# A ring of 2560 instead of 2304 tokens, and 512-token blocks in slots 48 to 143, in a fused window-attention and two-layer kernel

## The chip, the cores and the metric

The kernel runs on one core of a Trainium2 chip. The metric is the device time of one execution in microseconds; lower is better. The profile is of one execution, and its times are microseconds from the start of its span, unless marked ns.

## The reference

Attention with a window of 32 tokens to each side, over 8 batches of 8 heads, 576 tokens and 64 elements, and then two matrix products with an activation between them on the 8 x 576 = 4608 tokens of 512 elements. Inputs and output are float32.

```python
scores = np.matmul(q, k.transpose(0, 1, 3, 2)) / np.sqrt(64)      # 8, 8, 576, 576
mask = np.abs(pos[:, None] - pos[None, :]) <= 32
scores = np.where(mask, scores, -1e9)
attn = np.exp(scores - scores.max(-1, keepdims=True))
attn = attn / (attn.sum(-1, keepdims=True) + 1e-9)
x = np.matmul(attn, v).transpose(0, 2, 1, 3).reshape(4608, 512)
h = x @ w_in                                                      # 512 x 2048
g = np.where(h >= 1, h, np.where(h <= -1, 0, (h + 1) ** 2 / 4))
return g @ w_out                                                  # 2048 x 512
```

## The kernel before

All matmuls take bfloat16 and sum in float32. The order of the work is written out by hand: each engine runs its instructions in the order in which the Python loop emits them, and semaphores keep data right between engines.

**The main loop** (`for a in range(NF * NB + 2 * NF)`) has 160 slots; `a` is the slot. In slots 0 to 143 a slot makes one tile of 512 elements per partition of the hidden layer, in this order:

- TensorE projects into `hp`, a PSUM tile of the pool `ps_h`, which has two buffers. A *narrow* slot takes 256 tokens and 256 of the 2048 hidden features: 8 matmuls of 256 columns (in `project`, L488). A *wide* slot takes 512 tokens and 128 features: 4 matmuls of 512 columns (L513), over the planes `kk` of `xT` in the order 0, 2, 1, 3. Slots 56 to 135 are wide (`WIDE = 56, 136`), so eight narrow slots make one block of 256 tokens, and sixteen wide slots make two.
- ScalarE makes `rr` from `hp` (L532), VectorE makes `mx` from `hp` and `rr` (L538) and `gT` from `rr` and `mx` (L539). In a few early slots ScalarE makes `mx`. When both have read `hp`, its buffer is free, for the projection two slots on.
- TensorE multiplies `gT` of earlier blocks with `w_out` into `op` (`unit`, L448): from slot 40 on three matmuls of 512 columns a slot, from slot 72 on four; slots before 40 take a part of this work in another form. Each 16 of them end a tile of 128 tokens, which ScalarE copies to `osb` (L452) and SyncE's queue stores.

**The input of the projection** is `xT`, the attention's output, transposed: four planes of 128 partitions, plane `kk = 2a + y`. It is a ring of `RING = 4 * S` = 2304 tokens: token n stands at n modulo 2304. `gT` has four places for blocks of 256 tokens; the function `home` says which place a block takes, so that the two blocks of a wide pair, which begins at an odd block, stand at a fixed step from each other.

**The attention** is cut into *sessions*, which the function `at` hangs on slots; `run(a)` emits those of slot `a` after the slot's projection, `run(a + 0.5)` those of `a + 0.5` after the slot's `unit` matmuls. A batch has five sums, each paired with scores that are needed later (`steps`): plane parity `y1` = 0 and 1 of tokens 0 to 223, the same of tokens 224 to 479, and tokens 480 to 575 of both. The list `sl` gives the slots of the sessions from the second sums of batch 2 on: entry n holds sums number 6 + n and scores number 7 + n of the sequence that begins with batch 1. Sums of batch 3 are entries 4 to 8, those of batch 4 entries 9 to 13. In a session

- TensorE makes the sums (matmuls of `pt` with `ones` and `vn` into `bb`, L294). `bb` is of the pool `ps_n`, which has one buffer; then the scores (L228, L253), into the one buffer of `ps_s`.
- ScalarE takes Exp of the scores (L236, or L261 for a batch's last scores, which are fewer), then Ln and Exp of the sums, the reciprocal (L300, L301: `lr`, `rc`).
- VectorE masks the exponentials (L202), and multiplies `bb` with `rc` into `xT` (L306, L309). These multiplies are collected in `muls`, and `flush()` emits them at the start of the next slot, ahead of that slot's `mx`. The multiply is the last reader of `bb`.

In the slots that concern us the order on every engine is therefore: projection, `rr`, `mx`, `gT`, then the session, then `unit`; or `unit` ahead of the session where it hangs on a half.

**The loads** of batches 3 to 7 (q, k and v through GpSimd's queue, `load_nat` and `load_v`), and the transposes of q and k by DMA from SyncE's queue (`xpose`), hang on slots counted from `sl`: the loads 17 to 15 slots ahead of the session `sl[5 * (b - 1) - 7]`, the transposes 11 and 9 slots ahead of it.

Of the kernel before, what the change touches and what calls it, by code (L numbers as in the profile page):

```python
# [14 lines left out]
def kernel(  # L15
# [19 lines left out]
    nc = tc.nc  # L35
    B, H, S, D = q.shape
# [3 lines left out]
    NU = NY * S // 128  # L40
    MAIN = 480
    TAIL = S - MAIN
    RING = 4 * S
    PAD = 32
    WIDE = 56, 136
    LONG = 2

    const = ctx.enter_context(tc.tile_pool(name="const", bufs=1))
# [20 lines left out]
    w_out = const.tile([128, 16, DM], BF, name="w_out")  # L69
    xT = const.tile([128, NY, RING], BF, name="xT")  # L70
    gT = const.tile([128, 16, 4, 256], BF, name="gT")
# [3 lines left out]
    V, P, A = nc.vector, nc.gpsimd, nc.scalar  # L75
# [73 lines left out]
    w = [(load_w_in, c0, c1, h) for c0, c1 in zip(cuts, cuts[1:]) for h in range(2)]  # L149
# [114 lines left out]
    muls = []  # L264

    def sums(b, y1, lo, hi, pool=ps_n):

        bb = two_banks(pool)
        w = hi - lo
        todo = []  # L270
        if lo < MAIN:
            ys, D0 = (y1,), w
            for par in range(2):
                a0 = max(lo, 32 * par)
                off = 32 - 64 * par
                todo.append((None, a0 - lo, hi - lo, lambda a, h, par=par, a0=a0, off=off: (
                    pt[b][HD[a], h, y1, par, a0 + off:hi + off])))
                for c2 in range(4):
                    q0, q1 = max(0, 128 * c2 - off, lo), min(128 * c2 + 128 - off, hi)
                    if q0 < q1:  # L280
                        todo.append((NC * y1 + 2 * c2 + par, q0 - lo, q1 - lo, lambda a, h, par=par, q0=q0, q1=q1, off=off: (
                            pt[b][HD[a], h, y1, par, q0 + off:q1 + off])))
        else:
            ys, D0 = (0, 1), 2 * w
            todo.append((None, 0, 2 * w, lambda a, h: pt8[b][HD[a], h].rearrange("p y j -> p (y j)")))
            for y in ys:
                todo.append((NC * y + 8, y * w, y * w + w, lambda a, h, y=y: pt8[b][HD[a], h, y]))
                for c in (None, NC * y + 7):
                    todo.append((c, y * w, y * w + 64, lambda a, h, y=y: pt[b][HD[a], h, y, 1, 448:512]))
        for n, (c, c0, c1, p) in enumerate(todo):  # L290
            o = D0 if c is None else 0
            for a in range(2):
                for h in range(2):
                    nc.tensor.matmul(bb[HD[h], a, o + c0:o + c1], ones[HD[a]] if c is None else vn[b][HD[a], c, h],  # L294
                                     p(a, h), start=n == 0, stop=True, skip_group_check=True)

        def end():
            lr = smp.tile([128, 2, 256], FP, name="lr", bufs=1)
            rc = smp.tile([128, 2, 256], FP, name="rc")
            A.activation(lr[:, :, :D0], bb[:, :, D0:2 * D0], AF.Ln)  # L300
            A.activation(rc[:, :, :D0], lr[:, :, :D0], AF.Exp, scale=-1.0)  # L301
            r0 = (b * S + lo) % RING
            o = xT.rearrange("p (a y) t -> p a y t", a=2)[:, :, ys[0]:ys[-1] + 1, r0:r0 + w]
            if len(ys) == 1:
                o = o[:, :, 0]
                muls.append(lambda: V.tensor_mul(o, bb[:, :, :D0], rc[:, :, :D0]))  # L306
            else:
                like = "p a (y j) -> p a y j"
                muls.append(lambda: V.tensor_mul(o, bb[:, :, :D0].rearrange(like, y=2), rc[:, :, :D0].rearrange(like, y=2)))  # L309
        return end  # L310
# [68 lines left out]
    NF = DFF // 256  # L379
# [27 lines left out]
        at(a, seq[2 + n][0])  # L407
    for n, a in enumerate((18, 20, 26.5, 28)):
        at(a, seq[3 + n][1])
    sl = [30, 32, 35, 38, 41, 44, 47, 50, 52, 57, 60, 63, 66, 68, 72, 76, 79, 82, 86]  # L410
    sl += [90, 93, 96, 100, 104, 108, 111, 114, 118, 123]
    for n, a in enumerate(sl):
        at(a, seq[6 + n][0], seq[7 + n][1] if n < len(sl) - 1 else None)
    for t in range(2):
# [2 lines left out]
    for b in range(LONG + 1, B):  # L417
        a = sl[5 * (b - 1) - 7] - 17
# [4 lines left out]

    op = {}

    def home(t):

        return (3 - t % 4 if t % 4 in (0, 3) else t % 4) if WIDE[0] <= NF * t < WIDE[1] else t % 4

    def unit(x):  # L430

        tt, j = divmod(x, 16)
        if tt == NT // 128 - 1:
            half, n = divmod(j, 8)
            if n == 0:
                op[tt] = ps_o.tile([128, 256], FP, name="op", tag="op")
            cols = slice(256 * half, 256 * half + 256)
            for k in (2 * n, 2 * n + 1):
                nc.tensor.matmul(op[tt], gT[:, k, home(tt // 2), 128 * (tt % 2):128 * (tt % 2) + 128], w_out[:, k, cols],  # L439
                                 start=k == 0, stop=k == 15)  # L440
            if n == 7:
                osb = osp.tile([128, 256], FP, name="osb")
                A.copy(osb, op[tt])
                nc.sync.dma_start(out=out[128 * tt:128 * tt + 128, cols], in_=osb)
            return
        if j == 0:
            op[tt] = ps_o.tile([128, DM], FP, name="op", tag="op")
        nc.tensor.matmul(op[tt], gT[:, j, home(tt // 2), 128 * (tt % 2):128 * (tt % 2) + 128], w_out[:, j],  # L448
                         start=j == 0, stop=j == 15)
        if j == 15:  # L450
            osb = osp.tile([128, DM], FP, name="osb")
            A.copy(osb, op[tt])  # L452
            nc.sync.dma_start(out=out[128 * tt:128 * tt + 128, :], in_=osb)
# [40 lines left out]
    for a in range(NF * NB + 2 * NF):  # L494
        wide = WIDE[0] <= a < WIDE[1]
        eng = None if a < 14 else V
        post = [] if a >= 40 else [x for n, x in pairs if n == a] + [a - NF] * (a >= 2 * NF + 2)
        for b, x in loads.get(a, []):
            if x < 2:
                load_nat(b, x)  # L500
            else:
                for n in range(4):
                    load_v(b, n)
        if a == 0 or a > 3:
            flush()
        if a < NF * NB:
            if wide:
                n, f = divmod(a - WIDE[0], 2 * NF)
                t = WIDE[0] // NF + 2 * n
                r0 = TB * t % RING  # L510
                hp = ps_h.tile([128, 2, TB], FP, name="hp", tag="hp")
                for n, kk in enumerate((0, 2, 1, 3)):
                    nc.tensor.matmul(hp.rearrange("p n t -> p (n t)"), w_in[:, kk, 128 * f:128 * f + 128],  # L513
                                     xT[:, kk, r0:r0 + 2 * TB], start=n == 0, stop=n == 3)
                g = gT[:, f, home(t):home(t + 1) + 1:home(t + 1) - home(t)]
            else:
                t, f = divmod(a, NF)
                r0 = TB * t % RING
                if a in (0,):
                    hps = [ps_h.tile([128, 2, TB], FP, name="hp", tag="hp") for _ in range(2)]  # L520
                    for y in range(2):
                        for n in range(2):
                            project(hps[n], f + n, r0, [(j, y + 2 * m) for j in range(2) for m in range(2)], y == 0, y == 1)
                elif not hps:
                    pool, tag = (ps_o, "op") if a == 6 else (ps_h, "hp")
                    hps = [pool.tile([128, 2, TB], FP, name="hp", tag=tag)]
                    project(hps[0], f, r0, [(j, kk) for j in range(2) for kk in (0, 2, 1, 3)], True, True)
                hp = hps.pop(0)
                g = gT[:, 2 * f:2 * f + 2, home(t)]

            rr = ewp.tile([128, 2, TB], FP, name="rr")
            A.activation(rr, hp, AF.Relu, scale=0.5, bias=0.5)  # L532
            mx = ewp.tile([128, 2, TB], FP, name="mx")
            if a in two_on_act:
                A.activation(mx, rr, AF.Square)
                V.scalar_tensor_tensor(g, hp, 1.0, mx, op0=ALU.max, op1=ALU.min)
            else:
                V.tensor_max(mx, hp, rr)  # L538
                V.scalar_tensor_tensor(g, rr, 1.0, mx, op0=ALU.min, op1=ALU.mult)  # L539
        flush()  # L540
        run(a)
        for x in post:
            if x < 16:
                pair(x)
            else:
                for j in range(4):
                    unit(4 * x + j)
        if a >= 40:
            n = 3 if a < 72 else 4
            for x in range(done, done + n):  # L550
                unit(x)
            done += n
        run(a + 0.5)
        for x in xps.get(a, []):
            xpose(*x)
# [30 lines left out]
```

## Time and profile before

| what | us |
|---|---|
| five runs, median | 307.56 |
| five runs, lowest to highest | 306.9 to 308.48 |
| the profiled execution, its own time | 307.01 |
| its span in the profile | 305.2 |

Busy time by stage (the bounds are starts of slots: 20.42 of 25.00 means that TensorE worked in 20.42 of the 25 us):

| stage, us | length | TensorE | VectorE | ScalarE | GpSimd |
|---|---|---|---|---|---|
| 0 to 25, start | 25.00 | 20.42 | 12.44 | 16.46 | 21.18 |
| 25 to 63, to slot 24 | 38.00 | 37.58 | 31.08 | 28.14 | 14.40 |
| 63 to 98.7, to slot 42 | 35.70 | 34.65 | 31.14 | 24.32 | 14.78 |
| 98.7 to 123.2, slots 42 to 55 | 24.50 | 23.87 | 23.06 | 17.82 | 7.79 |
| 123.2 to 151.5, slots 56 to 71 | 28.30 | 27.50 | 26.69 | 20.37 | 10.44 |
| 151.5 to 273.9, slots 72 to 135 | 122.40 | 119.97 | 104.42 | 74.45 | 8.25 |
| 273.9 to 287.1, slots 136 to 143 | 13.20 | 13.09 | 10.68 | 5.35 | 0.00 |
| 287.1 to the end | 18.10 | 14.66 | 1.78 | 3.69 | 0.00 |

The granted TensorE clock is 1.00 in all stages but the last, where it is 0.99. Some matmul records are missing from the trace, mostly the first `op` matmul after a session, which shows as 0.16 us of idle time put down to "issue".

### The profile page before, as it was taken

What the parts mean: (1) busy time and instruction counts of PE and PEld (TensorE: products, weight loads), DVE (VectorE), ACT (ScalarE), POOL (GpSimd) and SP (SyncE); (2) the same over time, 40 slices, a digit from 0 to 9 for tenths busy, and PEclk for the clock granted to TensorE, in tenths of its full rate; (3) what the DMA queues carried; (4) which work ended last, traced back from release to release, by engine and by line L of the source; (5) the groups of instructions that cost most, each with busy time, mean ns of one, the idle gap of its engine ahead of it and who ended that gap; (6) DMA issues with size and microseconds to landing.
All of it is one profiled execution on the core that took longest, in us unless ns stands there. A gap on an engine that the chain in (4) does not pass through costs nothing.

```text
span 305.2 us, 7808 instructions
## 1 busy us (share of the span) xinstructions
PE 291.7 (96%) x3286; PEld 174.6 (57%) x3324; DVE 241.3 (79%) x378; ACT 190.6 (62%) x318; POOL 76.8 (25%) x92
## 2 busy tenths in 40 slices
PE   7889999999999999999999999999999999999995
PEld 3468878876666776554445444444445444446644
DVE  4278858888888999999988888988888888788700
ACT  3687796648757768668666766665667644444311
POOL 8796661028009106404600720000000000000000
PEclk9999999999999999999999999999999999999999
DMA  9999999999999999996999996551011000010121
GB/s 150 184 191 201 182 184 173 172 157 156 135 204 101 162 140 146 165 153 112 171 112 183 108 168 71 114 113 37 34 37 38 34 37 35 34 37 34 59 81 69
DMA packets 137171, 35.67 MB, mean 117 GB/s; under 512 B 122160, under 2 KB 132912, under 8 KB 137136
## 3 DMA queue, kind: packets, MB, share of 16 engines
q0 software_dynamic: 102976, 18.06, 79.2%
q1 hardware_dynamic: 34016, 16.81, 26.0%
q8 instruction: 26, 0.43, 0.6%
q10 hardware_dynamic: 144, 0.29, 0.4%
q14 instruction: 9, 0.07, 0.1%
HBM read 36.70 MB, written 9.44 MB: 151 GB/s over the span
## 4 chain that ended last, share of the span: by engine, by line
PE 89%; DMA 4%; POOL 3%; issue 2%; ACT 0%; POOLq 0%; ACTq 0%
PE op L448 34%; PE hp L513 23%; PE hp L488 17%; PE bb L294 6%; PE op L463 5%; DMA w_in<-in_moe_w_in_dram 2%; PE bb L228 2%; DMA qh<-in_q_dram 2%; POOL w_in L111 2%; PE op L439 1%; POOL vn L107 1%; PE tp L188 1%; POOL kh L86 0%; PE bb L207 0%; PE bb L253 0%
## 5 line engine op out<-in xcount | busy, mean ns | idle before, releaser
L532 ACT ACTIVATE rr<-hp 128x512 f32<-128x512 f32 x144 | 85.5, 595 | 84.5 <-PE hp L513 49.5
L448 PE MATMUL op<-w_out,gT 128*128 128x512 bf16 x460 | 119.5, 379 | 5.0 <-issue 4.8
L538 DVE TENSOR_TENSOR mx<-hp,rr 128x512 f32<-128x512 f32 x139 | 95.7, 689 | 26.7 <-ACT rr L532 25.1
L539 DVE SCALAR_TENSOR_TENSOR gT<-rr,mx 128x512 bf16<-128x512 f32 x139 | 96.2, 692 | 4.8
L513 PE MATMUL hp<-xT,w_in 128*128 128x512 bf16 x320 | 82.1, 379 | 0.0
L448 PEld LDWEIGHTS <-gT 128*128 128x128 bf16 x496 | 46.1, 98 | 47.6
L488 PE MATMUL hp<-xT,w_in 128*128 128x256 bf16 x512 | 66.2, 273 | 1.9 <-DMA w_in<-in_moe_w_in_dram 1.1
L488 PEld LDWEIGHTS <-w_in 128*128 128x128 bf16 x512 | 49.3, 98 | 16.9 <-issue 1.7
L513 PEld LDWEIGHTS <-w_in 128*128 128x128 bf16 x320 | 31.3, 98 | 37.8
L99 POOL DMA_DIRECT2D qn<-in_q_dram x12 | 14.6, 1223 | 91.1 <-DMA kT<-kn 89.0
L236 ACT ACTIVATE pt<-bb 128x1024 bf16<-128x1024 f32 (+1 forms) x33 | 32.9, 1002 | 4.7 <-PE bb L228 3.3
L306 DVE TENSOR_TENSOR xT<-bb,rc 128x512 bf16<-128x512 f32 (+1 forms) x32 | 21.0, 657 | 10.1 <-ACT rc L301 9.2
L107 POOL DMA_DIRECT2D vn<-in_v_dram x32 | 27.5, 894 | 5.2 <-DMA w_out<-in_moe_w_out_dram 2.9
L452 ACT COPY osb<-op 128x512 f32<-128x512 f32 x31 | 18.0, 582 | 12.5 <-PE op L448 12.1
L301 ACT ACTIVATE rc<-lr 128x512 f32<-128x512 f32 (+2 forms) x40 | 23.5, 587 | 1.3
L300 ACT ACTIVATE lr<-bb 128x512 f32<-128x512 f32 (+2 forms) x40 | 22.0, 550 | 0.5 <-PE bb L294 0.4
L202 DVE TENSOR_TENSOR pt<-pt,mask 128x1024 bf16<-128x1024 bf16 (+1 forms) x33 | 20.3, 614 | 0.5 <-ACT pt L236 0.5
L294 PE MATMUL bb<-pt,ones 64*64 64x256 bf16 (+3 forms) x352 | 19.4, 255 | 0.1
L294 PE MATMUL bb<-pt,vn 64*64 64x128 bf16 (+3 forms) x712 | 18.3, 204 | 0.2 <-DMA vn<-in_v_dram 0.2
L294 PEld LDWEIGHTS <-ones 64*64 64x64 bf16 x352 | 10.2, 106 | 12.5 <-issue 12.5
L294 PEld LDWEIGHTS <-vn 64*64 64x64 bf16 x712 | 16.7, 107 | 0.4 <-DMA vn<-in_v_dram 0.4
L463 PE MATMUL op<-w_out,gT 128*128 128x256 bf16 x128 | 16.3, 273 | 0.0
(61 smaller groups left out, 136.4 us busy)
## 6 DMA issues: line engine op xcount, KB each, us to landing
out_dram<-osb SPq DMA_DIRECT2D x35, 256.0 KB, 2.4
vn<-in_v_dram POOLq DMA_DIRECT2D x32, 144.0 KB, 11.2
qn<-in_q_dram POOLq DMA_DIRECT2D x12, 288.0 KB, 6.7
kn<-in_k_dram POOLq DMA_DIRECT2D x12, 288.0 KB, 8.8
w_in<-in_moe_w_in_dram POOLq DMA_DIRECT2D x12, 128.0 KB, 5.3
w_out<-in_moe_w_out_dram POOLq DMA_DIRECT2D x4, 256.0 KB, 7.9
w_out<-in_moe_w_out_dram POOLq DMA_DIRECT2D x2, 512.0 KB, 12.9
kh<-in_k_dram POOLq DMA_DIRECT2D x4, 144.0 KB, 5.3
```

Of the source, the lines that this page charges most:

```text
L107: nc.gpsimd.dma_start(out=vn[b][64 * a:64 * a + 64, :, h], in_=v[b, y:y + 2].rearrange("y s d -> (y s) d") .rearrange("(c r) d -> r c d", ...
L236: A.activation(p, ps[:, :, :w * n].rearrange(like, y=m), AF.Exp, scale=D ** -0.5)
L294: nc.tensor.matmul(bb[HD[h], a, o + c0:o + c1], ones[HD[a]] if c is None else vn[b][HD[a], c, h], p(a, h), start=n == 0, stop=True, skip_g ...
L300: A.activation(lr[:, :, :D0], bb[:, :, D0:2 * D0], AF.Ln)
L301: A.activation(rc[:, :, :D0], lr[:, :, :D0], AF.Exp, scale=-1.0)
L448: nc.tensor.matmul(op[tt], gT[:, j, home(tt // 2), 128 * (tt % 2):128 * (tt % 2) + 128], w_out[:, j], start=j == 0, stop=j == 15)
L463: nc.tensor.matmul(o[:, tt], gT[:, j, p, 128 * tt:128 * tt + 128], w_out[:, j, 256 * half:256 * half + 256], start=not done, stop=len(done ...
L488: nc.tensor.matmul(hp[:, j], w_in[:, kk, 256 * f + 128 * j:256 * f + 128 * j + 128], xT[:, kk, r0:r0 + TB], start=first and n == 0, stop=l ...
L513: nc.tensor.matmul(hp.rearrange("p n t -> p (n t)"), w_in[:, kk, 128 * f:128 * f + 128], xT[:, kk, r0:r0 + 2 * TB], start=n == 0, stop=n == 3)
L532: A.activation(rr, hp, AF.Relu, scale=0.5, bias=0.5)
L538: V.tensor_max(mx, hp, rr)
L539: V.scalar_tensor_tensor(g, rr, 1.0, mx, op0=ALU.min, op1=ALU.mult)
```

## The change

- The ring of `xT` has 2560 tokens (`RING = 4 * S + 256`), ten blocks of 256, so that pairs of blocks that begin at an even block never lie across its end. Batch 4, whose tokens 224 to 479 now do, has the multiplies into `xT` of that part (one for each `y1`) split in two: 32 tokens and 224.
- Slots 48 to 143 are wide (`WIDE = 48, 144`): the pairs are blocks 6 and 7, 8 and 9, up to 16 and 17. `home` goes, and a block's place in `gT` is its number modulo 4.
- Nine entries for sums of batches 2 to 4 in `sl`, 3 and 5 to 12, and entry 13 and entry 25 have other slots. Entry by entry, from n = 3: 38 to 39; 41 stays; 44 to 42.5; 47 to 44; 50 to 46; 52 to 53; 57 to 55; 60 to 57; 63 to 59.5; 66 to 61.5; 68 to 67. Entry 25 (batch 7, second sums of tokens 0 to 223): 111 to 110. Loads and transposes of batches 3 and 4 hang one slot later, those of batch 5 one slot earlier.

```diff
-    RING = 4 * S
+    RING = 4 * S + 256
     PAD = 32
-    WIDE = 56, 136
+    WIDE = 48, 144
...
             r0 = (b * S + lo) % RING
-            o = xT.rearrange("p (a y) t -> p a y t", a=2)[:, :, ys[0]:ys[-1] + 1, r0:r0 + w]
+            x = xT.rearrange("p (a y) t -> p a y t", a=2)[:, :, ys[0]:ys[-1] + 1]
             if len(ys) == 1:
-                o = o[:, :, 0]
-                muls.append(lambda: V.tensor_mul(o, bb[:, :, :D0], rc[:, :, :D0]))
-            else:
+                n = min(w, RING - r0)
+                for c0, c1 in ((0, n), (n, w)):
+                    if c0 < c1:
+                        r = (r0 + c0) % RING
+                        muls.append(lambda c0=c0, c1=c1, r=r: V.tensor_mul(
+                            x[:, :, 0, r:r + c1 - c0], bb[:, :, c0:c1], rc[:, :, c0:c1]))
+            else:
+                o = x[:, :, :, r0:r0 + w]
                 like = "p a (y j) -> p a y j"
...
-    sl = [30, 32, 35, 38, 41, 44, 47, 50, 52, 57, 60, 63, 66, 68, 72, 76, 79, 82, 86]
-    sl += [90, 93, 96, 100, 104, 108, 111, 114, 118, 123]
+    sl = [30, 32, 35, 39, 41, 42.5, 44, 46, 53, 55, 57, 59.5, 61.5, 67, 72, 76, 79, 82, 86]
+    sl += [90, 93, 96, 100, 104, 108, 110, 114, 118, 123]
...
-    def home(t):
-
-        return (3 - t % 4 if t % 4 in (0, 3) else t % 4) if WIDE[0] <= NF * t < WIDE[1] else t % 4
-
...
-        nc.tensor.matmul(op[tt], gT[:, j, home(tt // 2), 128 * (tt % 2):128 * (tt % 2) + 128], w_out[:, j],
+        nc.tensor.matmul(op[tt], gT[:, j, tt // 2 % 4, 128 * (tt % 2):128 * (tt % 2) + 128], w_out[:, j],
                          start=j == 0, stop=j == 15)
...
-                g = gT[:, f, home(t):home(t + 1) + 1:home(t + 1) - home(t)]
+                g = gT[:, f, t % 4:t % 4 + 2]
...
-                g = gT[:, 2 * f:2 * f + 2, home(t)]
+                g = gT[:, 2 * f:2 * f + 2, t % 4]
```

More of the change, by code (lines that the diff above doesn't have):

```diff
@@ L438, in unit @@
             for k in (2 * n, 2 * n + 1):
-                nc.tensor.matmul(op[tt], gT[:, k, home(tt // 2), 128 * (tt % 2):128 * (tt % 2) + 128], w_out[:, k, cols],
+                nc.tensor.matmul(op[tt], gT[:, k, tt // 2 % 4, 128 * (tt % 2):128 * (tt % 2) + 128], w_out[:, k, cols],
                                  start=k == 0, stop=k == 15)
```

## The prediction

> **What bounds the kernel now.** I read the page first (busy shares, the chain of waits), then the groups by line, then the timeline of each engine around slots 38 to 72, since the change touches the order only there and near slots 108 to 112. S(a) is the start of slot a's first `hp` matmul.
>
> ```profile
> PE 291.7 (96%) x3286; PEld 174.6 (57%) x3324; DVE 241.3 (79%) x378; ACT 190.6 (62%) x318; POOL 76.8 (25%) x92
> ...
> PE 89%; DMA 4%; POOL 3%; issue 2%; ACT 0%; POOLq 0%; ACTq 0%
> ```
>
> TensorE is busy nearly all the time and is 89% of the chain that ends last; the 4% DMA and 3% POOL of that chain lie before 25 us. TensorE's timeline:
>
> ```profile
> 98.72 1.04 PE L488 MATMUL hp<-xT,w_in 128*128 128x256 bf16 x8
> 99.59 0.81 PE L448 MATMUL op<-w_out,gT 128*128 128x512 bf16 x3
> 100.24 1.04 PE L488 MATMUL hp<-xT,w_in 128*128 128x256 bf16 x8
> ...
> 123.25 1.03 PE L513 MATMUL hp<-xT,w_in 128*128 128x512 bf16 x4
> 124.11 0.81 PE L448 MATMUL op<-w_out,gT 128*128 128x512 bf16 x3
> 124.76 1.03 PE L513 MATMUL hp<-xT,w_in 128*128 128x512 bf16 x4
> ```
>
> Read starts, not durations (ends are modelled). A narrow slot's projection takes 99.59 - 98.72 = 0.87, a wide one's 124.11 - 123.25 = 0.86; slots are 1.52 and 1.51 long. From 60 us to the tail matmul follows matmul at these distances, with 0.1 at each switch to or from a session's small matmuls (and records missing in places): TensorE waits for nobody there but for 0.1 at slot 32, so whatever newly holds it adds to the time one for one, and nothing later gives it back.
>
> VectorE is the near second. Around the session of slot 41 (ScalarE's, then VectorE's timeline):
>
> ```profile
> 98.18 1.02 ACT L236 ACTIVATE pt<-bb 128x1024 bf16<-128x1024 f32 x1
> 99.10 0.54 ACT L300 ACTIVATE lr<-bb 128x448 f32<-128x448 f32 x1
> 99.67 0.58 ACT L301 ACTIVATE rc<-lr 128x448 f32<-128x448 f32 x1
> 100.16 0.58 ACT L532 ACTIVATE rr<-hp 128x512 f32<-128x512 f32 x1
> ```
>
> ```profile
> 99.42 0.68 DVE L202 TENSOR_TENSOR pt<-pt,mask 128x1024 bf16<-128x1024 bf16 x1
> 100.28 0.63 DVE L306 TENSOR_TENSOR xT<-bb,rc 128x448 bf16<-128x448 f32 x1 [0.18 <-ACT rc L301]
> 100.82 0.68 DVE L538 TENSOR_TENSOR mx<-hp,rr 128x512 f32<-128x512 f32 x1
> 101.54 0.69 DVE L539 SCALAR_TENSOR_TENSOR gT<-rr,mx 128x512 bf16<-128x512 f32 x1
> 102.15 0.68 DVE L538 TENSOR_TENSOR mx<-hp,rr 128x512 f32<-128x512 f32 x1
> ```
>
> The session's first sums start at 97.35, its multiply into `xT` ends at 100.28 + 0.63 = 100.91: a chain of 3.56. A slot costs VectorE 102.15 - 100.82 = 1.33 of TensorE's 1.52. The 256-token session of slot 47 has a chain of 3.82 (sums 108.11, multiply 111.24 + 0.69), that of slot 50, with the small scores, 3.20 (113.57; 116.09 + 0.68). `ps_n` has one buffer, so the next session's first sums wait for that multiply. The closest spacing so far is 26.5 to 28:
>
> ```profile
> 70.26 0.56 DVE L309 TENSOR_TENSOR xT<-bb,rc 128x384 bf16<-128x384 f32 x1 [0.25 <-ACT rc L301]
> ```
>
> ```profile
> 67.50 0.28 PE L294 MATMUL bb<-pt,ones 64*64 64x192 bf16 x4
> ...
> 70.87 0.29 PE L294 MATMUL bb<-pt,ones 64*64 64x224 bf16 x4
> ```
>
> There the multiply ends at 70.82 and the next sums start 0.05 later, in slots that still have four `unit` matmuls (1.74 long). No cover is left, and the change puts sessions 1.5 slots apart where slots are 1.52 long.
>
> **What the Trainium skill says.** "TensorE: Matmul & The Clock Gate", Back-to-back issue gap: a warm matmul follows the one before by N/2.4 + 2.5 ns, so 109.2 ns at N = 256 and 215.8 at 512. The trace agrees: 0.87/8 = 109 and 0.86/4 = 216 ns. "Perfetto Trace Analysis", Per-engine timelines: ScalarE and VectorE are strict FIFO, and TensorE can only pull weight loads ahead of matmuls; so a held first sums matmul holds the projection behind it, and a session's Ln stands behind its scores' Exp (98.18, then 99.10 above). "VectorE: DVE Perf Modes", The TRN2 errata: an fp32 tensor_tensor takes (N+151)/0.96 ns, with N the elements per partition, a fixed cost paid per instruction. The trace has 691, 624 and 554 ns at 512, 448 and 384, against 691, 624 and 557.
>
> **The change part by part.**
>
> *Sixteen slots wide instead of narrow (48-55, 136-143).* 128 matmuls of 256 columns become 64 of 512: 16 x (8 x 109.2 - 4 x 215.8) = 16 x 10.4 ns = -0.17. 64 weight loads go too, but they hide (98 ns each beside 109 or 216). ScalarE and VectorE have the same tiles. Sum: -0.17.
>
> *Larger ring, other `gT` slots.* No instruction; overwritten blocks are read long before. 0. POOL and SP keep their order and issue counts; loads and transposes shift by one slot, but the loads are released by the transposes (91.1 us of POOL idle at L99), not by slots. 0.
>
> *Sessions 39 and 41.* 38 to 39 moves one session across a slot; S(40) stays 94.86 and slot 41 repeats the timeline above, perhaps 0.1 later on VectorE, as slot 39's copy of `osb` now stands in ScalarE behind that session's Ln and Exp. 0.
>
> *Session 42.5 (was 44).* From 41's first sums TensorE has: rest of that session 0.72 (97.35 to 98.07, the end of its scores being 98.72 less three units of 0.216), units 0.65, projection 0.87, units 0.65, switch 0.10: 2.99. It needs 3.56 + 0.04 signalling + up to 0.1: stall 0.65. Behind it on TensorE stand slot 43's projection and everything after. Bounds 0.4 to 0.8.
>
> *Session 44 (was 47).* From 42.5's sums: 0.72 + projection 0.87 + units 0.65 + projection 0.87 + switch 0.10 = 3.21, against 3.60: stall 0.40. Bounds 0.1 to 0.6.
>
> *Session 46.* From 44's sums 0.81 + 0.65 + 1.52 + 0.97 = 3.95, against 3.82 + 0.04. Fits by 0.09: 0; up to 0.2 if ScalarE lags.
>
> *Slot 48 now reads all of 46's output.* From 46's sums to S(48): 0.67 + 0.65 + 1.52 = 2.84. Its matmuls take kk in the order 0, 2, 1, 3; 46 writes planes 1 and 3, so the third is held, 2 x 0.216 later: 3.27. Needed 3.20 + 0.04 + about 0.15, since slots 45 and 46's `rr` and a copy stand late behind 44's chain: 3.39, stall 0.12. Bounds 0 to 0.4.
>
> *Sessions 53 to 61.5.* Two slots apart TensorE has 3.84 (0.72 + 0.65 + 1.51 + 0.96) against 3.60: they fit, but in those 3.84 VectorE owes two slots (2.66), a mask (0.60 to the next start, 73.41 to 74.01) and a multiply (0.54, 100.28 to 100.82), 3.80 in all, and stays backlogged. 59.5 to 61.5 gives 0.81 + 1.51 + 1.51 + 0.10 = 3.93. Its multiply is split by the ring's end (32 and 224 tokens). 64 elements at the slope of the three durations, 1.07 ns each from 554 at 384, is 212 ns, less the 0.08 by which neighbours overlap: +0.14. Needed 3.82 + 0.14 + 0.04 = 4.00: stall 0.07, bounds 0 to 0.4.
>
> *Slot 64.* Its `hp` takes the buffer that slot 62's `mx` frees, and that `mx` stands behind 61.5's multiplies. From 59.5's sums, the large multiply starts at 3.27 (3.82 - 0.69 + 0.14), then `mx` of 60 after 0.54, two slots 2.66, the small mask 0.26 (115.83 to 116.09), split multiplies 0.14 + 0.54, `mx` of 62 0.69 to its end: 8.10. TensorE gets there at 4.00 + 0.67 + 1.51 + 1.51 = 7.69: stall 0.41 + 0.04 = 0.45. Bounds 0 to 0.8.
>
> *Session 110 (was 111), read by slot 112's third matmul.* 0.72 + 0.86 + 1.73 + 0.43 = 3.74 against 3.60: 0. The other sessions from 67 on lie three slots or more apart, or stay where they were: 0.
>
> Sum: -0.17 + 0.65 + 0.40 + 0.12 + 0.07 + 0.45 = **+1.52**. On the profiled execution's 307.01 (span 305.2 plus 1.8 around it) that is 308.5; it lies 0.55 under the runs' median of 307.56, and as the result is a median I carry the difference over: **309.1**.
>
> **The rivals.**
>
> *Only the stall at 42.5 is real* (not slower by what can be told). Those at 44, 48, 61.5 and 64 hang on lags that I carried forward in a ledger. If VectorE's multiplies come some 0.4 earlier than that, TensorE waits once: 0.65 - 0.17 = +0.5, 308.0. It decides at stalls of 1.09 in all. For: each is under half a us. Against: the chains are measured, and 3.21 against 3.60 leaves little doubt at 44.
>
> *No stall*: 307.4. For: the kernel tolerates slack of under 0.1 us already. Against: the one-buffer `ps_n`.
>
> *Faster*: narrow slots cost TensorE more than starts show. Beyond 0.92 us it needs 58 ns a slot; the trace gives 10. About 306.3.
>
> *Worse*: all upper bounds together, 0.8 + 0.6 + 0.2 + 0.4 + 0.4 + 0.8 - 0.17 = +3.0, 310.6, if VectorE's backlog passes from one session to the next.
>
> **How the numbers follow.** Forecast 0.60, worse 0.09, only 42.5 0.18, none 0.07, faster 0.06. A difference under 0.3% (0.92 us) can't be told from no change. Slower 0.69, same 0.25, faster 0.06. The range runs from no stall (307.4) to the upper bounds (310.6); the forecast's own is 308.5 to 310.0.
>
> **What would show it.** TensorE idle before the sums (L294) of slots 42.5 and 44, near 0.65 and 0.4 us, released by VectorE's `xT` multiply; the third wide matmul of slot 48 late by 0.1; the first of slot 64 released by `mx`; 320 + 64 wide matmuls at an unchanged 216 ns. If the sums at 42.5 follow the units by 0.10, my reading of the `ps_n` buffer is wrong and the forecast falls; if S(44) - S(41) is under 6.6 (unstalled 2.34 + 2.34 + 1.52 = 6.20, forecast 6.85), it is too high.

## The result, and the profile after

| | before | after |
|---|---|---|
| median, us | 307.39 (80 runs) | 308.54 (43 runs) |
| lowest, us | 306.48 | 307.96 |
| the profiled execution: time and span, us | 307.01, 305.2 | 308.47, 306.7 |

The change makes the kernel slower: the ratio of after to before is 1.0032, with a 95% interval of 1.0023 to 1.0042. On 307.39 us that is +0.98 us, between +0.7 and +1.3. The two profiled executions differ by more, 1.46 us in time and 1.5 in span, and so do the lowest times, 1.48. That gap of half a us seems to have a cause of its own, which the later experiments look for. One execution of 614.78 us, of the kernel with both moves below, is left out of its ratio as a slow one.

The page of the changed kernel (busy time by engine; the chain that ended last, by engine):

```profile
PE 292.6 (95%) x3221; PEld 168.4 (55%) x3260; DVE 241.6 (79%) x380; ACT 190.3 (62%) x318; POOL 77.1 (25%) x92
...
PE 85%; POOL 3%; ACT 3%; issue 3%; DVE 2%; DMA 2%; ACTq 0%; POOLq 0%
```

VectorE and ScalarE, which had no visible share of the chain, now have 2% and 3% of it. TensorE's waits (who waited for whom: us in total, times, longest) have two new rows in the changed kernel:

```profile
PE bb L294 <- DVE xT L309: 0.9, 2, 0.6
...
PE hp L514 <- DVE mx L539: 0.2, 1, 0.2
```

They understate it, since a wait is counted only from the modelled end of the matmul before. TensorE's timeline of the changed kernel, read by starts, gives the full sizes:

```profile
99.50 0.81 PE L449 MATMUL op<-w_out,gT 128*128 128x512 bf16 x3
100.92 0.29 PE L294 MATMUL bb<-pt,ones 64*64 64x224 bf16 x4 [0.60 <-DVE xT L309]
...
103.16 1.04 PE L489 MATMUL hp<-xT,w_in 128*128 128x256 bf16 x8
104.52 0.30 PE L294 MATMUL bb<-pt,ones 64*64 64x256 bf16 x4 [0.33 <-DVE xT L309]
...
111.31 1.19 PE L514 MATMUL hp<-xT,w_in 128*128 128x512 bf16 x4
112.34 0.81 PE L449 MATMUL op<-w_out,gT 128*128 128x512 bf16 x3
...
135.27 0.81 PE L449 MATMUL op<-w_out,gT 128*128 128x512 bf16 x3
136.11 0.30 PE L294 MATMUL bb<-pt,ones 64*64 64x256 bf16 x4
...
139.16 0.81 PE L449 MATMUL op<-w_out,gT 128*128 128x512 bf16 x3
140.20 1.02 PE L514 MATMUL hp<-xT,w_in 128*128 128x512 bf16 x4 [0.24 <-DVE mx L539]
```

Three `unit` matmuls take 0.65 us, a switch to a session's small matmuls 0.10. So the sums of session 42.5 were due at 99.50 + 0.75 = 100.25 and came 0.67 later; those of 44, due 0.97 after the projection, 0.39 later. Slot 48's wide projection takes 1.03 instead of 0.86, 0.17 too long (its modelled length of 1.19 shows the hole within). Session 61.5's sums are 0.09 late, slot 64's projection 0.39. Together 1.71 us. VectorE's timeline of the changed kernel shows what was waited for:

```profile
100.24 0.62 DVE L309 TENSOR_TENSOR xT<-bb,rc 128x448 bf16<-128x448 f32 x1
...
103.85 0.62 DVE L309 TENSOR_TENSOR xT<-bb,rc 128x448 bf16<-128x448 f32 x1 [0.35 <-ACT rc L301]
...
111.18 0.68 DVE L309 TENSOR_TENSOR xT<-bb,rc 128x512 bf16<-128x512 f32 x1
111.78 0.68 DVE L539 TENSOR_TENSOR mx<-hp,rr 128x512 f32<-128x512 f32 x1
...
135.21 0.76 DVE L309 TENSOR_TENSOR xT<-bb,rc 128x64 bf16<-128x64 f32 x2 [0.41 <-ACT rc L301]
...
138.80 0.75 DVE L309 TENSOR_TENSOR xT<-bb,rc 128x64 bf16<-128x64 f32 x2
139.47 0.68 DVE L539 TENSOR_TENSOR mx<-hp,rr 128x512 f32<-128x512 f32 x1
```

The multiplies end at 100.86 and 104.47, and the sums follow 0.06 and 0.05 later. The multiply of 46 ends at 111.86, within slot 48's projection, and the split one of 61.5 pushes slot 62's `mx` to end at 140.15, 0.05 ahead of slot 64's projection.

### The profile page after: what moved, and what is told of

The parts are those of the page before. It is cut to its first block, busy times and chain, and to the rows that moved or that the text cites. A ratio compares the mean times of both kernels' runs of the same rounds, so it can differ in the third digit from the quotient of the medians.

```text
span 306.7 us, 7682 instructions
## 1 busy us (share of the span) xinstructions
PE 292.6 (95%) x3221; PEld 168.4 (55%) x3260; DVE 241.6 (79%) x380; ACT 190.3 (62%) x318; POOL 77.1 (25%) x92
## 4 chain that ended last, share of the span: by engine, by line
PE 85%; POOL 3%; ACT 3%; issue 3%; DVE 2%; DMA 2%; ACTq 0%; POOLq 0%
PE op L449 33%; PE hp L514 26%; PE hp L489 11%; PE bb L294 6%; PE op L464 5%; PE bb L228 2%; DMA w_in<-in_moe_w_in_dram 2%; POOL vn L107 1%; PE op L440 1%; POOL w_in L111 1%; DVE xT L309 1%; PE tp L188 1%; ACT rr L533 1%; ACT pt L236 1%; POOL kh L86 1%
## 5 line engine op out<-in xcount | busy, mean ns | idle before, releaser
L514 PE MATMUL hp<-xT,w_in 128*128 128x512 bf16 x378 | 98.2, 379 | 0.5 <-DVE mx L539 0.2
L514 PEld LDWEIGHTS <-w_in 128*128 128x128 bf16 x384 | 37.4, 98 | 45.6 <-issue 0.8
L489 PE MATMUL hp<-xT,w_in 128*128 128x256 bf16 x384 | 49.6, 273 | 1.7 <-DMA w_in<-in_moe_w_in_dram 1.2
L489 PEld LDWEIGHTS <-w_in 128*128 128x128 bf16 x384 | 36.6, 98 | 12.0 <-issue 1.5
L309 DVE TENSOR_TENSOR xT<-bb,rc 128x448 bf16<-128x448 f32 (+2 forms) x34 | 21.1, 627 | 9.6 <-ACT rc L301 8.8
```

Source lines behind the costliest of these rows:

```text
L309: muls.append(lambda c0=c0, c1=c1, r=r: V.tensor_mul(x[:, :, 0, r:r + c1 - c0], bb[:, :, c0:c1], rc[:, :, c0:c1]))
L489: nc.tensor.matmul(hp[:, j], w_in[:, kk, 256 * f + 128 * j:256 * f + 128 * j + 128], xT[:, kk, r0:r0 + TB], start=first and n == 0, stop=l ...
```

## The experiments

Theory: the sessions' new slots make TensorE wait, at 42.5 and 44 for the one buffer of `bb`, at 48 and 64 behind VectorE; the wide slots themselves bring 10 ns each, and the ring nothing. Rivals: the wide slots or the ring cost in themselves; narrow slots cost much more than their starts show. A third theory came with the gap between profiles and runs: before, some executions wait for a transpose by DMA. All times are beside runs of the kernel before on the same chip; ratios are to those, with their 95% intervals in brackets.

### The new session slots alone

```diff
-    sl = [30, 32, 35, 38, 41, 44, 47, 50, 52, 57, 60, 63, 66, 68, 72, 76, 79, 82, 86]
-    sl += [90, 93, 96, 100, 104, 108, 111, 114, 118, 123]
+    sl = [30, 32, 35, 39, 41, 42.5, 44, 46, 53, 55, 57, 59.5, 61.5, 67, 72, 76, 79, 82, 86]
+    sl += [90, 93, 96, 100, 104, 108, 110, 114, 118, 123]
```

> The kernel before with the changed kernel's list of session slots, nothing else: ring of 2304, slots 56 to 135 wide. Theory (the sessions, not the wide slots, make the loss, by waits on the one buffer of bb and on VectorE): TensorE idle before the sums of 42.5 and 44 as in the changed kernel (0.67 and 0.39 us beyond the switch of 0.10), no wait at slot 48, which is narrow and reads older tokens, and at slot 64 a wait on mx that is 0.14 shorter for want of the split multiply, about 0.25. Sum about +1.3 us against before. Rival (the loss comes with the wide slots 48 to 63, which read the attention's output at once, or with the ring and its split multiplies): within 0.3 us of before.

Ratio 1.0019 (1.0003 to 1.0036); span 306.7 us. Its TensorE timeline:

```profile
99.63 0.81 PE L448 MATMUL op<-w_out,gT 128*128 128x512 bf16 x3
101.04 0.29 PE L294 MATMUL bb<-pt,ones 64*64 64x224 bf16 x4 [0.60 <-DVE xT L306]
...
103.29 1.04 PE L488 MATMUL hp<-xT,w_in 128*128 128x256 bf16 x8
104.65 0.30 PE L294 MATMUL bb<-pt,ones 64*64 64x256 bf16 x4 [0.33 <-DVE xT L306]
...
139.09 0.81 PE L448 MATMUL op<-w_out,gT 128*128 128x512 bf16 x3
140.11 1.02 PE L513 MATMUL hp<-xT,w_in 128*128 128x512 bf16 x4 [0.21 <-DVE mx L538]
```

With the old ring and the old wide slots the same waits stand at the same places: 0.66 at 42.5, 0.39 at 44, 0.37 at slot 64, where I had expected 0.25; none at slot 48, and none before the sums of 61.5. The span is as long as the changed kernel's: the sessions alone make the loss that the traces show. Over the runs the loss is 0.6 us (0.1 to 1.1), under the 1.3 that I expected; this list has the moves to slots 39 and 53 in it, to which the last experiments come back.

### No wide slots at all

```diff
-    WIDE = 56, 136
+    WIDE = 0, 0
```

> The kernel before with no wide slot at all: 80 wide slots become narrow. Theory (a narrow projection costs TensorE 8 x 109.2 ns against 4 x 215.8 ns, 10.4 ns a slot): 80 x 10.4 ns = +0.83 us, and projections 0.87 us apart from their units in all slots. Rival (a narrow slot costs much more than the starts of matmuls show, so that the widening was worth a good part of a us and the sessions cost that much more): over +2 us. Rival (a narrow slot costs nothing extra): 0.

Ratio 1.0031 (1.0012 to 1.0050), that is +0.95 us, 0.4 to 1.5, for 80 slots. Its TensorE timeline in what were wide slots:

```profile
264.93 1.04 PE L488 MATMUL hp<-xT,w_in 128*128 128x256 bf16 x8
265.80 1.03 PE L448 MATMUL op<-w_out,gT 128*128 128x512 bf16 x4
266.66 1.04 PE L488 MATMUL hp<-xT,w_in 128*128 128x256 bf16 x8
```

A narrow projection takes 0.87 there too, and the units 0.86. The two scores of slot 41, at 97.73 before and 98.37 here, tell that 0.64 of the 1.45 us by which the spans differ arose earlier, ahead of the slots that the edit changes; the remaining 0.81 is 80 times 10 ns. The earlier part comes from a wait in slot 38 for the transpose of batch 3's k by DMA:

```profile
91.68 0.20 PE L294 MATMUL bb<-pt,vn 64*64 64x64 bf16 x4
92.54 0.42 PE L228 MATMUL bb<-qT,kT 64*64 64x128 bf16 x16 [0.66 <-DMA kT<-kn]
```

Up to slot 55 this kernel does what the kernel before does, so the kernel before can wait there too. The widening of 16 slots is worth 0.17 us, and both rivals about wide and narrow slots fall.

### The other buffer for the sums of 42.5

```diff
-        at(a, seq[6 + n][0], seq[7 + n][1] if n < len(sl) - 1 else None)
+        p, s = ((ps_s,), (ps_n,)) if n == 5 else ((), ())
+        at(a, (*seq[6 + n][0], *p), (*seq[7 + n][1], *s) if n < len(sl) - 1 else None)
```

> The changed kernel, in whose session 42.5 the sums take the buffer of ps_s and the scores that of ps_n. Theory (the waits at 42.5 and 44 are for the one buffer of bb): sums of 42.5 start 0.10 after the units; its scores, 0.38 later, wait for the multiply of session 41 some 0.27 us; the sums of 44 find ps_n free long ago and its scores find ps_s free, so no wait at 44. 1.06 us of waiting become 0.27: 0.8 us faster than the changed kernel, about +0.2 to +0.7 against before. Rival (what holds TensorE there is ScalarE's or VectorE's whole backlog, through hp or gT): the waits move to the next projections, and the time stays within 0.2 us of the changed kernel's.

Ratio 1.0018 (1.0004 to 1.0032), against the changed kernel's 1.0032 from other runs. Its TensorE timeline:

```profile
100.19 0.81 PE L450 MATMUL op<-w_out,gT 128*128 128x512 bf16 x3
101.07 0.29 PE L294 MATMUL bb<-pt,ones 64*64 64x224 bf16 x4
...
101.61 0.42 PE L228 MATMUL bb<-qT,kT 64*64 64x128 bf16 x16
...
103.49 1.04 PE L490 MATMUL hp<-xT,w_in 128*128 128x256 bf16 x8
104.46 0.30 PE L294 MATMUL bb<-pt,ones 64*64 64x256 bf16 x4
...
107.43 1.04 PE L490 MATMUL hp<-xT,w_in 128*128 128x256 bf16 x8
108.71 0.30 PE L294 MATMUL bb<-pt,ones 64*64 64x256 bf16 x4 [0.24 <-DVE xT L309]
...
111.55 1.27 PE L515 MATMUL hp<-xT,w_in 128*128 128x512 bf16 x4
112.66 0.81 PE L450 MATMUL op<-w_out,gT 128*128 128x512 bf16 x3
```

At 42.5 the sums are 0.13 late instead of 0.67 and at 44 not at all (104.46 is 0.97 after 103.49): the one buffer was what held TensorE there. The scores of 42.5, which now take that buffer, come 0.54 after the sums instead of 0.38, 0.16 late. But 46, which had fitted, now waits 0.31, and slot 48 0.25 (1.11 for 0.86). Over half of what the buffer gave back turns into other waits: behind the buffer stands VectorE, which has five sessions to digest between slots 39 and 48. In slots 42.5 to 48 TensorE waits 0.85 instead of 1.23. So the theory holds for the place and the rival for part of the gain, 0.4 us instead of 0.8. The intervals of the two ratios overlap, so the runs don't prove that gain. The span, 307.0 us, doesn't speak against it: in that execution TensorE comes to slot 42 at 99.32, 0.69 later than in the changed kernel's, before the two differ. The 0.13 that is left before the sums of 42.5 was not traced further.

### Sessions 59.5 and 61.5 at 59 and 61

```diff
-    sl = [30, 32, 35, 39, 41, 42.5, 44, 46, 53, 55, 57, 59.5, 61.5, 67, 72, 76, 79, 82, 86]
+    sl = [30, 32, 35, 39, 41, 42.5, 44, 46, 53, 55, 57, 59, 61, 67, 72, 76, 79, 82, 86]
```

> The changed kernel with sessions 59.5 and 61.5 at 59 and 61. Theory (slot 64's projection waits for mx of slot 62, which stands behind the split multiply of the last session): that multiply comes some 0.65 us earlier against slot 64, so the wait of 0.39 us there falls below 0.1, with the 0.09 before the sums of 61 as they are; 0.3 to 0.4 us faster than the changed kernel, waits at 42.5, 44 and 48 unchanged. Rival (slot 64's wait is for VectorE's total load in slots 53 to 63): the wait stays at 0.3 to 0.4.

Ratio 1.0025 (1.0011 to 1.0038); span 306.4 us, 0.3 less than the changed kernel's. Its TensorE timeline:

```profile
130.45 1.03 PE L514 MATMUL hp<-xT,w_in 128*128 128x512 bf16 x4
131.56 0.30 PE L294 MATMUL bb<-pt,ones 64*64 64x256 bf16 x4
...
139.28 0.81 PE L449 MATMUL op<-w_out,gT 128*128 128x512 bf16 x3
139.93 1.03 PE L514 MATMUL hp<-xT,w_in 128*128 128x512 bf16 x4
```

Slot 64's projection follows its units by 0.65: its wait of 0.39 is gone, so it hung on the place of the last session. Session 59 is now 0.15 late (1.11 for 0.96), two slots behind 57, and 61 0.09 as before. The ratio's interval overlaps the changed kernel's; the trace carries this verdict.

### Even distances of two slots

```diff
-    sl = [30, 32, 35, 39, 41, 42.5, 44, 46, 53, 55, 57, 59.5, 61.5, 67, 72, 76, 79, 82, 86]
+    sl = [30, 32, 35, 38, 40, 42, 44, 46, 53, 55, 57, 59, 61, 67, 72, 76, 79, 82, 86]
```

> The changed kernel with its sessions of slots 39 to 61.5 at even distances of two slots: 38, 40, 42, 44, 46, then 53, 55, 57, 59, 61. Theory (the loss is the distance of 1.5 slots and the half-slot sessions before a wide pair, not the wide slots or the ring): two slots leave TensorE 3.84 us from one session's sums to the next against a chain of 3.60, so no wait at 42 and 44; at slot 48 the third wide matmul still waits 0.1 to 0.3 us for 46's multiply, and at 61 and 64 together at most 0.2. Waits fall from 1.7 to 0.2 to 0.5 us, the time to within 0.3 us of before. Rival (wide slots 48 to 63 need more of VectorE and ScalarE than they have, however the sessions lie): the waits turn up at other slots and the loss stays above 1 us.

Ratio 0.9995 (0.9981 to 1.0008). With ring and wide slots of the changed kernel, no loss can be told from none. In its trace 42 and 44 don't wait; 0.17 stands at slot 48, 0.15 at 59 and 0.09 at 61. The trace holds one more wait, the one that the trace without wide slots has:

```profile
91.99 0.20 PE L294 MATMUL bb<-pt,vn 64*64 64x64 bf16 x4
92.46 0.42 PE L228 MATMUL bb<-qT,kT 64*64 64x128 bf16 x16 [0.27 <-DMA kT<-kn]
```

The scores of slot 38 wait for the transpose of batch 3's k by DMA.

### The wait for the transposes: three moves in the kernel before

The kernel before has its first scores of batch 3 in slot 38 and those of batch 4 in slot 52; the change has them in 39 and 53. The loads and transposes of the batch hang one slot later with the session. This hardly moves them: in all the traces the transpose of batch 3's and of batch 4's q starts 0.15 or 0.16 us after the load that it reads has landed. I tried each of these moves alone, both, both a second time, and the opposite of the first.

```diff
-    sl = [30, 32, 35, 38, 41, 44, 47, 50, 52, 57, 60, 63, 66, 68, 72, 76, 79, 82, 86]
+    sl = [30, 32, 35, 39, 41, 44, 47, 50, 53, 57, 60, 63, 66, 68, 72, 76, 79, 82, 86]
```

Slot 38 to 39 alone:

> The kernel before with one session moved from slot 38 to 39, which is a part of the change. Before, the scores of slot 38 start at 91.9 us, and the load that waits for the same transpose of batch 3's k starts at 92.16. Theory A (the move is worth nothing): within 0.1 us of before. Theory B (in some executions the transpose lands after the scores want it and the kernel before loses some tenths of a us there, which the changed kernel does not, so that its loss over many runs, 1.0 us, is smaller than that of the two profiled executions, 1.5 us): 0.2 to 0.5 us faster than before.

Slot 52 to 53 alone:

> The kernel before with one session moved from slot 52 to 53, a part of the change. Theory C (before, the scores of slot 52 start 0.56 us after the load that waits for the transpose of batch 4's k was let go, 117.69 and 117.13, so in executions in which the transposes land later TensorE waits there, and the changed kernel, which comes 2.6 us later, does not): lowest time as before, 306.5, upper quartile down from 308.1 to about 307.5, ratio near 0.998. Rival (the spread of the kernel before comes from the loads of the first 25 us, which all kernels share): same spread and median as before.

Both, and both again:

> The kernel before with both moves, 38 to 39 and 52 to 53. Theory C with both transposes: median about 306.9 to 307.1 and a spread between quartiles as narrow as the changed kernel's, 0.6 us, ratio 0.997 to 0.999. Rival (spread from the start): no different from before.

> The kernel before with sessions 38 and 52 at 39 and 53, a second time, beside the next two on one chip. Theory C (TensorE waits in part of the executions of before for the transposes of k, and the two moves take that away): ratio again 0.996 to 0.999, lowest time that of before. Rival (the first result was chance): 1.000.

Slot 38 to 37:

> The kernel before with the session of slot 38 at 37. Theory C: the scores of batch 3 are wanted at about 90.2 us, and the transpose of its k lands between 91.6 and 92.5, so the wait that before has in part of its executions is seen in this one's trace, 1.4 to 2.3 us ahead of the scores (L228); TensorE then comes to slot 52 that much later and never waits for batch 4's transpose. Together +0.6 to +1.6 us against before's median. Rival (the transposes are not what TensorE can wait for): no wait, within 0.2 us of before.

| kernel | ratio to before | 95% interval |
|---|---|---|
| 38 to 39 | 0.9999 | 0.9982 to 1.0016 |
| 52 to 53 | 0.9995 | 0.9982 to 1.0008 |
| both | 0.9973 | 0.9961 to 0.9986 |
| both, again | 0.9990 | 0.9977 to 1.0004 |
| 38 to 37 | 1.0062 | 1.0039 to 1.0084 |

Theory B, of the first move alone, and theory C, of the second alone, aren't confirmed, and aren't refuted either: neither ratio can be told from 1, and both intervals reach down to a gain of 0.55 us. The medians are 0.51 and 0.35 lower than those of the kernel before beside them. Both moves together gain 0.8 us (0.4 to 1.2) in one set of runs and 0.3 (-0.1 to 0.7) in the other; the two intervals overlap between 0.4 and 0.7. The lowest times stay, 306.42 and 306.58 beside 306.42 and 306.44, and the middle half of the runs narrows, to 0.44 and 0.76 us beside 0.85 and 1.18: what the moves take away is in part of the executions only.

The trace of the opposite move shows the wait in plain sight. TensorE's timeline with the session at slot 37, and GpSimd's, whose next load is let go by the same transpose:

```profile
90.19 0.20 PE L294 MATMUL bb<-pt,vn 64*64 64x64 bf16 x4
92.57 0.42 PE L228 MATMUL bb<-qT,kT 64*64 64x128 bf16 x16 [2.17 <-DMA kT<-kn]
```

```profile
93.09 2.45 POOL L99 DMA_DIRECT2D qn<-in_q_dram  x2 [17.26 <-DMA kT<-kn]
```

TensorE stands still for over 2 us until the transpose lands, as expected. The loss in nine runs, 1.9 us (1.2 to 2.6), is larger than the 0.6 to 1.6 that I expected. GpSimd's load starts 0.52 after the scores that had waited, so its start tells the landing about half a us late. The profile of the kernel before has the same two:

```profile
91.92 0.40 PE L228 MATMUL bb<-qT,kT 64*64 64x128 bf16 x16
```

```profile
92.16 2.45 POOL L99 DMA_DIRECT2D qn<-in_q_dram  x2 [17.07 <-DMA kT<-kn]
```

There the transpose landed at about 91.6, 0.3 us ahead of its use. In the thirteen kept traces GpSimd's load starts between 92.16 and 93.50; in eight it is later than 92.45, so that the transpose landed later than 91.92, when the kernel before wants it. The rival, that the spread comes from the kernel's start, accounts for less: slot 32's projection, ahead of both uses, starts between 78.28 and 78.59 in twelve of the traces and at 79.08 in one.

For batch 4 compare GpSimd's load and TensorE's scores in the kernel before,

```profile
117.13 2.45 POOL L99 DMA_DIRECT2D qn<-in_q_dram  x2 [16.71 <-DMA kT<-kn]
```

```profile
117.69 0.40 PE L228 MATMUL bb<-qT,kT 64*64 64x128 bf16 x16
```

with the same two in the kernel with both moves, and the load in that kernel's second trace:

```profile
119.46 2.44 POOL L99 DMA_DIRECT2D qn<-in_q_dram  x2 [18.31 <-DMA kT<-kn]
```

```profile
119.22 0.40 PE L228 MATMUL bb<-qT,kT 64*64 64x128 bf16 x16
```

```profile
117.24 2.45 POOL L99 DMA_DIRECT2D qn<-in_q_dram  x2 [16.55 <-DMA kT<-kn]
```

In two executions of one kernel the load was let go 2.2 us apart. Here it starts about 0.67 after the landing (119.93 and 120.60 in the trace of the next version, whose scores wait). So the transpose landed about 1.2 us ahead of the scores in the profile of before, and about 0.4 ahead in the first execution with both moves; scores at 117.69 would have waited about 1.1 there.

So the wait itself is shown, at slot 38 in the very order of the kernel before. How often it comes, and how much of the gap of half a us it makes, is argued from the spread and the landings, not measured. Whether both moves are needed stays open.

### A version with wide slots and both cures

```diff
-    sl = [30, 32, 35, 39, 41, 42.5, 44, 46, 53, 55, 57, 59.5, 61.5, 67, 72, 76, 79, 82, 86]
+    sl = [30, 32, 35, 38.5, 40, 42, 44, 46, 53, 55, 57, 59, 61, 67, 72, 76, 79, 82, 86]
...
-        a = sl[5 * (b - 1) - 7] - 17
+        a = int(sl[5 * (b - 1) - 7]) - 17
```

> The changed kernel with sessions 38.5, 40, 42, 44, 46, 53, 55, 57, 59, 61: two slots apart almost everywhere, and batch 3's scores 0.9 us later than in slot 38. Theory: waits of about 0.17 at slot 48, 0.2 to 0.3 before 59 and 61, none for a transpose in most executions, less 0.17 for the wide slots: 0.1 to 0.7 us faster than before, and 0.1 to 0.3 slower than the kernel before with its two moves. Rival (wide slots 48 to 63 cost in themselves): slower than before.

Ratio 0.9977 (0.9964 to 0.9991): 0.7 us faster than before (0.3 to 1.1), and so faster than both kernels, with the ring and the wide slots of the change. Its lowest time, 306.66, is not below that of the kernel before, 306.44: in its trace 0.41 us of waits stand at slots 48, 59 and 61, more than the 0.17 that the wide slots bring. The gain is in the other executions. The cure is not complete either, for the scores of batch 4 still wait in slot 53:

```profile
119.52 0.20 PE L294 MATMUL bb<-pt,vn 64*64 64x64 bf16 x4
119.93 0.42 PE L228 MATMUL bb<-qT,kT 64*64 64x128 bf16 x16 [0.21 <-DMA kT<-kn]
```

Beside it on the same chip the two moves alone had 0.9990, with the lower median, 307.22 against 307.40; the intervals overlap, so which of the two is better stays open.

## Why the prediction was right

**The waits.** The ledger of chains against distances named all five places. Forecast and measured in the changed kernel's trace: 42.5: 0.65 and 0.67; 44: 0.40 and 0.39; slot 48: 0.12 and 0.17; 61.5: 0.07 and 0.09; slot 64: 0.45 and 0.39. That is 1.69 against 1.71. Sessions 46 and 110, costed at nothing, don't wait. S(44) - S(41) was forecast at 6.85 and is 103.16 - 96.29 = 6.87.

**The wide slots.** -0.17 forecast; 80 slots made narrow cost 0.81 by the traces and 0.95 (0.4 to 1.5) by the runs, so 16 are worth 0.16 to 0.19. The section of the Trainium skill that the formula is from ("TensorE: Matmul & The Clock Gate", Back-to-back issue gap) calls it the gap of an isolated matmul and gives about 131 ns for N = 512 in a stream. The traces have 216 ns in a stream, 0.86 us for four, and this decides.

**The split multiply.** It was forecast at 0.14 more than an unsplit one and takes half of that: VectorE's next instruction starts 139.47 - 138.80 = 0.67 after it, against 111.78 - 111.18 = 0.60 after the unsplit one of 46. On the other side the sums of 61.5 follow the end of 59.5's split multiply by 136.11 - 135.97 = 0.14, where 0.04 was put down and 0.05 and 0.06 stand at 42.5 and 44; why is open. The two misses nearly cancel, so that 0.07 came so close to 0.09 is in part luck.

**The sum.** +1.52 forecast against +1.5 between the two spans. The sign and the mechanism hold: the loss came with the session slots alone, and spacing the sessions evenly takes it away.

**The term that was mis-sized.** Over many runs the loss is 0.98 us, two thirds of the forecast and at the lower edge of "slower by more than can be told". The median, 308.54, lies just inside the forecast's own range, 308.5 to 310.0, and 0.56 under 309.1; 0.17 of that is the five runs' median of before, 307.56, which came down to 307.39. I wrote that loads and transposes cost 0, and put sessions 39 and 53 down at nothing, as slot 41 keeps its time in the profiled execution. That is so where the transposes land in time. They don't always, and then the kernel before waits and the changed kernel mostly doesn't: the two moves, which are part of the change, gave -0.8 and -0.3 us by themselves, and 1.5 less such a gain is what the runs show. The hint was in the profile of before: the transpose of batch 3's k landed only 0.3 us ahead of the scores at 91.92. Such a margin on a DMA should have been a term with its own bounds, below nothing.

**The rivals.** "Only the stall at 42.5" gave +0.5, or 308.0. By the time alone it is as near to the result as the forecast is: the loss of 0.98 lies 0.48 above the one and 0.54 under the other. The traces decide, for all the waits that the rival denies are there.

## What to carry to other kernels

When one engine runs without a gap, a reordering is priced by a ledger: for each instruction that could be held, the time that the busy engine takes to get there against the measured chain that sets it free; tenths of a us add up, and the narrow margins decide. A single buffer sets the least distance between its users, and a second one only pays as far as the next engine in line has room. Look for margins on DMAs as well: a transfer that lands 0.3 us before its use in one profiled execution can land after it in others, and a change that moves the use shows in the median and not in the trace of such an execution.

## What the runs showed of the hardware

The same transposes by DMA land at different times from execution to execution: in two traces of one kernel, the one with both moves, the load behind batch 4's k was let go at 119.46 and at 117.24 us. TensorE, by contrast, repeats itself to a few hundredths: 0.66 and 0.67, 0.39 and 0.39 us of waiting at the same two sessions in two kernels.
